# A gated recurrence feeding an attention mixture: mixing two experts per float32 product, the loads of V cut in halves, a shorter warm-up

## The chip, the cores and the metric

The kernel runs on one core of one Trainium2 chip. The metric is the device time of one execution in microseconds (us), the median of several runs. Five engines work side by side and meet at semaphores: PE (matrix products; its weight loads are listed as PEld), DVE (vector), ACT (scalar), POOL (a second, slower vector engine) and SP, which here only issues DMA transfers, in order.

## The reference

Six arrays of 4 batches x 8 heads x 768 steps x 40 go through a recurrence, and its output through a mixture of four attention experts of which each token takes two:

```
for t in range(S):                       # 768 steps, state 40 x 40 for each of 32 heads
    y[:, :, t] = rt @ state
    Sa = state @ at
    state = state * wt - outer(Sa, bt) + outer(vt, kt)
x = y as (4, 768, 320)
logits = x @ w_gate                      # 4 experts, the best 2 of each token
for e in range(4):
    q, k, v = x @ wq[e], x @ wk[e], x @ wv[e]          # 64 columns each
    a = softmax(causal(q @ k.T / 8))
    out += gate[e] * (a @ v @ wo[e])
```

## The kernel before

**Recurrence.** Time is cut into 24 chunks of 32 steps, and heads into 4 groups of 8, which makes 96 units (chunk `c`, group `g`). A unit has seven pieces, `s_k s_v s_g s_y s_f s_u s_t`, and the main loop runs over steps `n`: step n runs piece `k` of unit n+3, `v` of unit n-1, `g` of n, `y` of n-3, `f` of n-2, `u` of n and `t` of n-3, in that order (`MAIN`). Between the pieces stand jobs that a table places at a step and a slot: `prep` (scans and products that prepare decay factors, 24 of them, named by letters) and `invert` (32x32 triangular inverses on DVE and POOL, through DRAM). `R1` and `R2` hold operands of two chunks in turn. Rows 0 to 31 of both take V of the chunk from DRAM: `load_c(c, 0)` fills `R1` (read by `s_g`), `load_c(c, 1)` fills `R2[:, 0]` (read by `s_v` and `s_y`) and two more operands, `RB` and `RT`. Both are issued on SP at the end of steps n = 4m and 4m+2 for chunk m+1.

**Prologue.** Before the main loop `warm()` issues products on PE that nobody reads and four DVE operations on `LT`; then the line `START` prepares the first units and the first inverse.

**Mixture of experts.** `proj` makes queries, keys, values (`VV`) and gates of a batch, `unit(b, j, e, last)` handles 256 queries of expert `e`: `scores`, `transp` (PE transposes the weights, ACT and DVE bring them to `PT`), `mix` (PE multiplies `VV` with `PT` into `ot`), `fin` (output projection with float32 `WO`). Values and weights are held as a high and a low part of the type fp32r: `VV` has both side by side in 128 columns, `PT` has two tiles, so that a unit takes two products per block of keys and an addition afterwards (L841, L842). The order of units is the table `UNITS`; unit n+0 is scored, n-3 transposed, n-4 mixed and n-6 finished in one step (`LAG`), and `ORDER` says how these are interleaved. Work that waits a few slots goes through `later`.

## Time and profile before

| | |
|---|---|
| median of 3 runs | 747.99 us (745.74 to 750.92) |
| the profiled execution, its own time | 750.69 us |
| its span, first to last instruction | 748.8 us |
| busy: PE, DVE, ACT, POOL | 652.5, 583.1, 513.1, 335.6 us |
| mean granted clock of PE | 0.95 |

Busy time is the union of an engine's instructions; an engine that is 87% busy over the whole span may be the limit in one stage and wait in another, so the stages are read one by one. Three can be told apart: the prologue up to about 97 us, the recurrence to 490 us, the mixture to the end. A float32 product appears as two matmul records, an fp32r product as one.

### The profile page before, as it was taken

The page shows a single profiled execution, that of the slowest core. Times are in us where ns is not written, and L with a number is a line of the kernel's source. Part 1 is how long each engine was busy: PE and PEld are TensorE (multiplying, and loading weights), DVE is VectorE, ACT ScalarE, POOL GpSimd, SP SyncE. Part 2 cuts the span into 40 slices and gives each one's busy share as a digit, 9 for nine tenths or more (in the row PEclk, how much of TensorE's full clock was granted, in tenths as well). Part 3 has the DMA queues.
Part 4 walks back from the last instruction along what each step waited for, and adds up shares of the span by engine and source line. Part 5 has one row for each costly group of instructions (what it writes and reads, how often), then busy time and mean ns, then how long its engine had stood idle before and what let it go on. Part 6 is the DMA issues. An engine that isn't in the chain of part 4 may idle for free.

```text
span 748.8 us, 25460 instructions
## 1 busy us (share of the span) xinstructions
PE 652.5 (87%) x10321; PEld 600.2 (80%) x10321; DVE 583.1 (78%) x1436; ACT 513.1 (69%) x1270; POOL 335.6 (45%) x514
## 2 busy tenths in 40 slices
PE   6650699999899889988999999979979989999997
PEld 6540589888899879877999999967868878798785
DVE  8899869877886797789568344369999899789894
ACT  4697267667677776666567767627757768678784
POOL 4466368318803861486048002022555344523541
PEclk9565599999999999999999999999999999999999
DMA  7750634584478357834641661143213112111101
GB/s 197 192 141 15 131 105 117 126 190 124 110 162 220 82 126 158 204 90 111 126 138 58 140 188 49 49 130 95 47 47 103 50 33 75 57 40 43 37 19 57
DMA packets 87413, 78.27 MB, mean 105 GB/s; under 512 B 54392, under 2 KB 72568, under 8 KB 87288
## 3 DMA queue, kind: packets, MB, share of 16 engines
q1 hardware_dynamic: 87144, 76.47, 40.7%
q8 instruction: 83, 1.36, 0.8%
q14 instruction: 42, 0.34, 0.2%
q10 hardware_dynamic: 144, 0.10, 0.1%
HBM read 56.10 MB, written 14.16 MB: 94 GB/s over the span
## 4 chain that ended last, share of the span: by engine, by line
PE 54%; DVE 19%; DMA 10%; ACT 6%; issue 3%; SPq 1%; POOL 0%; DVEq 0%; ACTq 0%; POOLq 0%
DMA R<-in_VT 8%; PE ps L357 6%; PE ps L381 6%; PE ps L407 5%; PE ps L363 5%; PE ps L374 4%; PE ps L350 4%; PE ps L280 4%; PE ot L836 4%; PE pt L711 3%; PE sc L791 3%; PE pt L821 3%; PE pt L847 3%; PE ps L368 3%; DVE TP L310 3%
## 5 line engine op out<-in xcount | busy, mean ns | idle before, releaser
L813 POOL TENSOR_TENSOR P<-P,m 128x128 f32<-128x128 f32 (+2 forms) x96 | 89.2, 951 | 115.6 <-DVE m L809 53.7
L396 DVE TENSOR_TENSOR XT<-ps,SC 40x128 f32<-40x128 f32 x192 | 55.2, 287 | 76.7 <-ACT R L391 67.2
L312 POOL TENSOR_TENSOR MT<-MT,TP 128x58 f32<-128x58 f32 (+26 forms) x170 | 86.7, 510 | 13.3
L280 PE MATMUL ps<-AB,KB 104*64 104x64 f32 x768 | 63.1, 249 | 27.3 <-DVE PC L260 12.8
L364 ACT ACTIVATE R<-ps 32x320 f32<-32x320 f32 x96 | 41.0, 427 | 66.2 <-PE ps L363 66.1
L280 PEld LDWEIGHTS ps<-AB,KB 104*64 104x64 f32 x768 | 58.3, 163 | 28.8 <-POOL AB L267 13.7
L802 ACT ACTIVATE P<-sc,m 128x128 f32<-128x128 f32 (+2 forms) x96 | 60.9, 635 | 29.9 <-DVE m L801 19.2
L381 PE MATMUL ps<-R,LS 128*40 128x80 f32 x1536 | 75.8, 236 | 4.3 <-DVE R L375 4.1
L363 PE MATMUL ps<-GT,TT 128*33 128x40 f32 x1536 | 73.4, 205 | 3.7 <-DMA TT<-Td 1.5
L407 PE MATMUL ps<-CM,R 128*40 128x40 f32 x1472 | 75.9, 209 | 0.0
L363 PEld LDWEIGHTS ps<-GT,TT 128*33 128x33 f32 x1536 | 65.8, 115 | 4.9 <-ACT GT L358 2.8
L791 PE MATMUL sc<-ks,qs 128*128 128x384 f32 (+4 forms) x256 | 62.5, 346 | 4.7 <-ACT P L802 4.0
L836 PE MATMUL ot<-pt,vv 128*128 128x256 f32 (+1 forms) x384 | 60.3, 289 | 6.5 <-DVE ots L842 6.0
L407 PEld LDWEIGHTS ps<-CM,R 128*40 128x40 f32 x1472 | 64.6, 122 | 1.0 <-issue 0.9
L825 DVE TENSOR_TENSOR pt<-pt,pt 128x384 fp32r<-128x384 f32 (+1 forms) x96 | 58.9, 618 | 5.3 <-ACT pt L824 3.6
L381 PEld LDWEIGHTS ps<-R,LS 128*40 128x40 f32 x1536 | 58.1, 117 | 5.7 <-DVE R L375 5.2
L374 PE MATMUL ps<-RB,VU 128*64 128x64 f32 x768 | 61.2, 224 | 0.0
L836 PEld LDWEIGHTS ot<-pt,vv 128*128 128x128 f32 x384 | 50.8, 189 | 10.9 <-DVE ots L842 8.9
L801 DVE TENSOR_REDUCE m<-sc 128x1 f32<-128x128 f32 (+2 forms) x96 | 58.7, 614 | 0.6
L824 ACT ACTIVATE pt<-pt 128x384 fp32r<-128x384 f32 (+1 forms) x96 | 52.0, 544 | 10.0 <-PE pt L821 8.5
L821 PE MATMUL pt<-CM,P 128*128 128x128 f32 x336 | 52.9, 275 | 3.8 <-DVE qs L720 2.6
L368 PE MATMUL ps<-CM,R 66*80 66x66 f32 x384 | 38.7, 223 | 18.4 <-DMA R<-in_VT 17.8
(153 smaller groups left out, 1657.5 us busy)
## 6 DMA issues: line engine op xcount, KB each, us to landing
R<-in_VT SPq DMA_DIRECT2D x48, 160.0 KB
RB<-in_RB SPq DMA_DIRECT2D x24, 320.0 KB
EK<-in_EK SPq DMA_DIRECT2D x18, 416.0 KB
ks<-ks SPq DMA_DIRECT2D x32, 192.0 KB
R<-in_RT SPq DMA_DIRECT2D x24, 200.0 KB
EW<-in_EA SPq DMA_DIRECT2D x18, 214.5 KB
xT<-XT SPq DMA_DIRECT2D x48, 80.0 KB
out_dram<-o SPq DMA_DIRECT2D x24, 160.0 KB
```

Of the source, the lines that this page charges most:

```text
L280: T.matmul(p_a[:, p, cc, :], kb[0:104, n, :], AB[0:104, n, :], start=True, stop=True)
L312: lambda: e.tensor_tensor(o, o, tmp, op=OP.add)]
L363: T.matmul(p_u[:, h], tt[:, o:o + 33], gt[:, h, :], start=True, stop=True)
L368: T.transpose(p_t[:, p], r2[0:66, 0, h0 + 2 * p:h0 + 2 * p + 2, :].rearrange("q h d -> q (h d)"), ident[0:66, 0:66])
L374: T.matmul(p_f[:, 2 * p:2 * p + 2], vu[:, p, :], rb[:, 4 * g + p, :], start=True, stop=True)
L381: T.matmul(p_y[s][64 * s:64 * s + 40, p], ls[:, h, :], r2[:, :, h, :], start=True, stop=True, tile_position=(0, 64 * s))
L407: T.matmul(p_t[64:104, h], rn[:, h0 + h, :], ident[:, 64:104], start=True, stop=True, tile_position=(0, 64))
L791: T.matmul(ps[:, c, 0:cw], QS[b][:, e, o], KS[b][:, e, z, k], start=(z == 0), stop=(z == 1 and not last), skip_group_check=True)
L802: later(DE, lambda: A.activation(pv, ps[:, 0:ch, 0:cw], AF.Exp, bias=m[:, 0, t:t + 1], accum_out=m[:, 1, t:t + 1]))
L813: PL.tensor_tensor(P[:, 0:n], P[:, 0:n], m[:, 3, t:t + 1].to_broadcast([128, n]), op=OP.mult)
L821: T.transpose(p[:, 128 * y:128 * y + 128], st["P"][t][:, 128 * c:128 * c + 128], ident)
L836: T.matmul(po[:, 128:256] if one else po, VV[b][:, k, e].rearrange("p a b -> p (a b)"), PT[:, 256 * k:256 * k + (128 if one else 256)], st ...
```

## The change

Three things change. `warm()` keeps its first 48 products and drops the others and its four DVE operations. `load_c` has a third part, k == 2, which fills heads 0 to 15 of `R2`, and k == 1 fills heads 16 to 31; the loop issues parts 2 and 0 right after piece `y` of step 4m and part 1 right after `y` of step 4m+2. In the mixture `VV` and `PT` become plain float32, the two experts of a pair are mixed together, each into 64 of the 128 partitions of `ot` (`tile_position`), and one copy on DVE replaces L841 and L842. The copy to `PT` is on ACT for even blocks and on DVE for odd ones, without a low part. `UNITS` keeps pairs of experts adjacent, and a mix runs only at the second of a pair, all blocks in one go.

```diff
@@ load_c
+        if k == 2:
+            nc.sync.dma_start(R2[c % 2][0:32, 0, 0:16].rearrange("p h d -> p (h d)"), I["VT"][c, :, 0:640])
         if k == 1:
-            nc.sync.dma_start(R2[c % 2][0:32, 0].rearrange("p h d -> p (h d)"), I["VT"][c])
+            nc.sync.dma_start(R2[c % 2][0:32, 0, 16:32].rearrange("p h d -> p (h d)"), I["VT"][c, :, 640:1280])
@@ seq
-                load_c(int(z[1]), int(z[2]))
+                for k in (0,) if z[2] == "0" else (2, 1):
+                    load_c(int(z[1]), k)
@@ warm
-        z = [ps([128, 512]) for _ in range(4)]
...
-        run(48, lambda k: mm(128, 40, 80, 0, 64 * (k % 2), k % 2))
...
-        run(12, lambda k: mm(40, 40, 72, 64 * (k % 2), 64 * (k % 2), 0))
...
-        V.transpose(tv.rearrange("p (a b) -> p a b", a=4), c[:, None, :].to_broadcast([128, 4, 128]))
-        V.transpose(tv.rearrange("p (b a) -> p a b", a=16), c[:, None, 0:32].to_broadcast([128, 16, 32]))
-        V.memset(tv, 1.5)
-        V.reciprocal(tv, tv)
+        z = [ps([128, 512]) for _ in range(2)]
+        for k in range(48):
+            T.matmul(z[k % 2][64 * (k % 2):64 * (k % 2) + 40, 0:80], CM[:, 0:40], CM[:, 0:80], start=True, stop=True,
+                     tile_position=(0, 64 * (k % 2)))
@@ main loop, inside the loop over the pieces x of step n
-        if n >= 4:
-            if n % 4 == 0:
-                load_c(n // 4 + 1, 0)
-            if n % 4 == 2:
-                load_c(n // 4 + 1, 1)
+            if x == "y" and n >= 4:
+                for k in ((2, 0), (), (1,), ())[n % 4]:
+                    load_c(n // 4 + 1, k)
@@ proj, vg
-        VV[b] = sp.tile([128, 6, 4, 2, 64], FR, name="vv", bufs=2)
+        VV[b] = sp.tile([128, 6, 4, 64], F32, name="vv", bufs=2)
...
-                later(DL, lambda: V.tensor_tensor(v[:, :, 1], pv, f32(v[:, :, 0]), op=OP.subtract))
@@ unit, transp
-                st["PT"] = [sp.tile([128, 12, 128], FR, name=f"pt{x}", bufs=2) for x in range(2)]
+                PT[b, j, e] = sp.tile([128, 12, 128], F32, name="pt", bufs=4)
...
-            A.activation(h, p[:, 0:n], AF.Copy)
-            later(DL, lambda: V.tensor_tensor(l, p[:, 0:n], f32(h), op=OP.subtract))
+            if z % 2:
+                V.tensor_copy(o, p[:, 0:n])
+            else:
+                A.activation(o, p[:, 0:n], AF.Copy)
@@ unit, mix
-                for x in range(2):
-                    PT = st["PT"][x].rearrange("p a b -> p (a b)")
-                    T.matmul(po[:, 128:256] if one else po, VV[b][:, k, e].rearrange("p a b -> p (a b)"),
-                             PT[:, 256 * k:256 * k + (128 if one else 256)], start=(k == 0 and x == 0), stop=(one and x == 1),
-                             skip_group_check=True)
+                for s in range(2):
+                    h = slice(64 * s, 64 * s + 64)
+                    P = PT[b, j, 2 * ep + s].rearrange("p a b -> p (a b)")
+                    T.matmul(po[h, 128:256] if one else po[h], VV[b][:, k, 2 * ep + s], P[:, 256 * k:256 * k + (128 if one else 256)],
+                             start=(k == 0), stop=one, tile_position=(0, 64 * s), skip_group_check=True)
             if one:
                 ot = OT[b, j]
-                later(1, lambda: A.activation(ot[q, ep], po[64:128], AF.Copy))
-                later(2, lambda: V.tensor_tensor(ot[q, ep], po[0:64], ot[q, ep], op=OP.add))
+                later(1, lambda: V.tensor_copy(ot[:, ep], po))
```

Line numbers of the changed file: L836 is L818 there, L821 is L800, L791 is L770, L847 is L827, L711 is L692, L794 is L773, L336 and L337 are L338 and L339, and the halves of `R2` are L335 (first) and L337 (second).

DVE at the start of the program, before (`LT` is the tile that the four dropped operations write, `EW` the first input of the recurrence):

```order
L217 MEMSET D1P_83 104x528
L218 MEMSET AB_119 128x1024
L221 MEMSET FL 128x48
L500 STREAM_TRANSPOSE LT_125<-CM 128x512
L501 STREAM_TRANSPOSE LT_125<-CM 128x16x32
L502 MEMSET LT_125 128x512
L503 RECIPROCAL LT_125<-LT_125 128x512
L258 SCALAR_TENSOR_TENSOR SUF_84<-EW_80,D_78 104x528
```

DVE at the same place, after:

```order
L217 MEMSET D1P_83 104x528
L218 MEMSET AB_119 128x1024
L221 MEMSET FL 128x48
L258 SCALAR_TENSOR_TENSOR SUF_84<-EW_80,D_78 104x528
L260 COPY PC_85<-SUF_84 104x4
```

The first scan (L258) now follows the memsets directly.

SP in steps 4 to 8, before (`R_133` and `R_134` are the two buffers of `R1`, `R_135` and `R_136` those of `R2`; `EW`, `EK`, `EA` are inputs of `prep`):

```order
L199 DMA EK_82<-in_EK 104x1024
L199 DMA EA_81<-in_EA 104x512
L333 DMA R_133<-in_VT 32x1280
L199 DMA EW_80<-in_EA 104x528
L199 DMA EK_82<-in_EK 104x1024
L335 DMA R_135<-in_VT 32x1280
L336 DMA RB_139<-in_RB 80x1024
L337 DMA R_135<-in_RT 40x1280
L199 DMA EA_81<-in_EA 104x512
L199 DMA EW_80<-in_EA 104x528
L333 DMA R_134<-in_VT 32x1280
```

SP at the same place, after:

```order
L199 DMA EK_82<-in_EK 104x1024
L199 DMA EA_81<-in_EA 104x512
L335 DMA R_135<-in_VT 32x640
L333 DMA R_133<-in_VT 32x1280
L199 DMA EW_80<-in_EA 104x528
L199 DMA EK_82<-in_EK 104x1024
L337 DMA R_135<-in_VT 32x640
L338 DMA RB_139<-in_RB 80x1024
L339 DMA R_135<-in_RT 40x1280
L199 DMA EA_81<-in_EA 104x512
L335 DMA R_136<-in_VT 32x640
L333 DMA R_134<-in_VT 32x1280
```

The first half of `R2` now stands ahead of the load of `R1` and of two loads for `prep`; the second half keeps the place of the whole.

PE in the mixture, one unit of 256 queries with six blocks of keys, before (`pt_9831` and `pt_9832` are the high and the low tile of one expert):

```order
L821 MATMUL pt<-CM,P 128x128 x3
L836 MATMUL ot<-pt_9831,vv 128x256
L836 MATMUL ot<-pt_9832,vv 128x256
L836 MATMUL ot<-pt_9831,vv 128x256
L836 MATMUL ot<-pt_9832,vv 128x256
L836 MATMUL ot<-pt_9831,vv 128x256
L836 MATMUL ot<-pt_9832,vv 128x256
L836 MATMUL ot<-pt_9831,vv 128x256
L836 MATMUL ot<-pt_9832,vv 128x256
L836 MATMUL ot<-pt_9831,vv 128x256
L836 MATMUL ot<-pt_9832,vv 128x256
L836 MATMUL ot<-pt_9831,vv 128x128
```

PE in the mixture, a pair of experts with six blocks, after:

```order
L800 MATMUL pt<-CM,P 128x128 x3
L818 MATMUL ot<-pt,vv 64x256 x10
L818 MATMUL ot<-pt,vv 64x128 x2
L770 MATMUL sc<-ks,qs 128x320 x4
L773 LDWEIGHTS BF_6823
L773 MATMUL sc<-BF_6823 128x128
```

Twelve products on 64 partitions each now serve two experts, where twelve on 128 partitions served one.

## Rows read from the trace of the kernel before

**Rows 1.** The profile page: busy time and share of the span of each engine.

```profile
PE 652.5 (87%) x10321; PEld 600.2 (80%) x10321; DVE 583.1 (78%) x1436; ACT 513.1 (69%) x1270; POOL 335.6 (45%) x514
```

**Rows 2.** Busy time of each engine in stretches of the span (start and end in us, then the length, the engines, the granted clock, the DMA share and GB/s): the prologue, the recurrence, the mixture, and four stretches of 40 us inside the recurrence.

```profile
0.00:97.00 97.00, 50.81 (x696) 46.43 (x696) 87.57 (x189) 58.63 (x90) 49.45 (x65) 0.65 0.56 134
97.00:490.00 393.00, 367.19 (x8009) 348.45 (x8008) 274.24 (x664) 272.34 (x703) 176.02 (x327) 0.99 0.52 127
490.00:748.70 258.70, 234.52 (x1621) 205.30 (x1617) 221.31 (x584) 182.17 (x477) 110.16 (x122) 1.00 0.21 59
160.00:200.00 40.00, 35.92 (x763) 33.78 (x761) 31.40 (x70) 27.36 (x72) 31.24 (x50) 0.96 0.56 146
240.00:280.00 40.00, 34.77 (x763) 32.32 (x760) 34.41 (x81) 29.37 (x79) 31.28 (x58) 1.00 0.48 118
280.00:320.00 40.00, 36.34 (x796) 34.94 (x798) 28.31 (x63) 26.23 (x65) 12.87 (x18) 1.00 0.76 178
320.00:360.00 40.00, 33.91 (x718) 31.88 (x713) 35.14 (x79) 26.11 (x71) 27.27 (x48) 0.96 0.40 102
```

**Rows 3.** Instructions of DVE, SP and ACT in the first 20 us, in order of time (start, length, engine and line).

```profile
4.38 0.71 DVE L500 STREAM_TRANSPOSE LT<-CM 128x512 f32<-128x512 f32 x1 [1.40 <-DMA CM<-in_CM]
5.13 1.05 DVE L501 STREAM_TRANSPOSE LT<-CM 128x512 f32<-128x512 f32 x1
6.87 3.35 DVE L503 RECIPROCAL LT<-LT 128x512 f32<-128x512 f32 x1
10.14 1.19 DVE L258 TENSOR_TENSOR_SCAN SUF<-EW,D 104x528 f32<-104x528 f32 x1
15.36 1.24 DVE L258 TENSOR_TENSOR_SCAN TT<-R,D 104x528 f32<-104x528 f32 x1
...
4.79 0.31 SPq L199 DMA_DIRECT2D LS<-in_EA  x1
6.35 0.31 SPq L199 DMA_DIRECT2D R<-in_EA  x1
...
8.02 0.72 ACT L255 ACTIVATE JK<-EW,CM 104x512 fp8e4<-104x512 f32 x1
```

**Rows 4.** Waits (who waited for whom: us in total, times, longest): two of the whole span, then that of PE for the load of `R2` between 240 and 280 us and between 320 and 360 us.

```profile
PE ps L368 <- DMA R<-in_VT: 17.8, 10, 2.7
SPq L335 <- PE ps L381: 42.6, 5, 10.7
...
PE ps L368 <- DMA R<-in_VT: 4.7, 2, 2.7
PE ps L368 <- DMA R<-in_VT: 4.4, 2, 2.3
```

**Rows 5.** One of these waits in order of time: SP issues the whole load of `R2`, PE runs `s_k` (L350) and then waits to start `s_v` (L368).

```profile
188.61 0.35 SPq L335 DMA_DIRECT2D R<-in_VT  x1
...
190.93 0.55 PE L350 MATMUL ps<-CM,KB 104*64 104x104 f32 x4
194.19 0.40 PE L368 MATMUL ps<-CM,R 66*80 66x66 f32 x4 [2.71 <-DMA R<-in_VT]
```

**Rows 6.** The stretch behind that wait and the one after it: the columns of rows 2.

```profile
195.20:198.60 3.40, 3.40 (x58) 3.40 (x53) 2.73 (x8) 1.45 (x4) 2.93 (x7) 0.52 0.43 120
198.70:202.10 3.40, 3.40 (x81) 3.25 (x79) 2.88 (x8) 2.32 (x7) 2.82 (x8) 0.99 0.07 11
```

**Rows 7.** Groups of instructions of the mixture (490 to 749 us), shapes apart: busy us and mean ns of one, then idle time before them and its releaser. DVE first, then ACT, then PE.

```profile
L825 DVE TENSOR_TENSOR pt<-pt,pt 128x512 fp32r<-128x512 f32 x48 | 32.8, 685 | 1.7 <-ACT pt L824 0.7
L825 DVE TENSOR_TENSOR pt<-pt,pt 128x384 fp32r<-128x384 f32 x48 | 26.5, 551 | 3.6 <-ACT pt L824 2.9
L842 DVE TENSOR_TENSOR ots<-ot,ots 64x256 f32<-64x256 f32 x48 | 19.9, 415 | 4.8 <-ACT ots L841 3.9
L735 DVE TENSOR_TENSOR vv<-pt,vv 128x256 fp32r<-128x256 f32 x24 | 10.0, 420 | 1.3 <-ACT gg L734 0.9
...
L824 ACT ACTIVATE pt<-pt 128x512 fp32r<-128x512 f32 x48 | 28.6, 597 | 6.2 <-PE pt L821 5.6
L824 ACT ACTIVATE pt<-pt 128x384 fp32r<-128x384 f32 x48 | 23.6, 491 | 3.8 <-PE pt L821 2.9
L841 ACT ACTIVATE ots<-ot 64x256 f32<-64x256 f32 x48 | 18.3, 381 | 2.6 <-PE ot L836 1.3
...
L836 PE MATMUL ot<-pt,vv 128*128 128x256 f32 x288 | 51.7, 302 | 6.5 <-DVE ots L842 6.0 <-DVE gm L764 0.4
L847 PE MATMUL pt<-wo,ots 128*128 128x320 f32 x96 | 30.9, 443 | 0.0
L836 PE MATMUL ot<-pt,vv 128*128 128x128 f32 x96 | 16.3, 250 | 0.0
```

**Rows 8.** PE in order of time, in runs without a gap (start, from the first start to the last end, line, count): an fp32r mix, a float32 output projection, float32 products at the tile positions (0, 0) and (0, 64) in turn, unread products of 40 rows x 72 columns at the positions (0, 0) and (64, 64) in turn into one PSUM bank, and a change from 80 weight columns to 33.

```profile
692.67 1.59 PE L836 MATMUL ot<-pt,vv 128*128 128x256 f32 x12
650.76 1.24 PE L847 MATMUL pt<-wo,ots 128*128 128x320 f32 x4
126.90 0.72 PE L381 MATMUL ps<-R,LS 128*40 128x80 f32 x15
12.28 0.93 PE L487 MATMUL ps<-CM 40*40 40x72 f32 x24
138.11 0.40 PE L368 MATMUL ps<-CM,R 66*80 66x66 f32 x4 [0.68 <-DMA R<-in_VT]
138.44 0.33 PE L357 MATMUL ps<-R,GLe 128*33 128x40 f32 x4
```

**Rows 9.** The chain of work that ended last, inside the mixture: shares by line for 490 to 560 us, then for 560 to 735 us.

```profile
by line: ACT P L802 13.5%; issue 12.0%; DVE m L801 10.9%; DVE qs L720 6.5%; DMA x<-xT 5.9%; PE pt L711 4.5%; DVE vv L735 3.9%; DVE ks L720 3.6%; DVE xh L688 3.5%; DVE pt L825 3.5%; DVE gr L751 2.8%; DVE gr L753 2.5%; DVE gm L765 2.4%; DVE o
by line: PE ot L836 14.3%; PE sc L791 12.6%; PE pt L821 12.1%; PE pt L711 12.0%; PE pt L847 8.9%; PE pt L730 5.1%; issue 4.7%; DVE m L801 4.0%; ACT P L802 3.0%; DVE pt L825 2.9%; DVE qs L720 2.6%; DVE ots L842 2.6%; DVE m L807 2.0%; DMA x<-
```

More of the change, by code (lines that the diff above doesn't have):

```diff
@@ L479, in warm @@
     def warm():
-        z = [ps([128, 512]) for _ in range(4)]
-        c = CM[:, 0:128]
-        tv = LT.rearrange("p a b -> p (a b)")[:, 0:512]
-        def run(n, f):
-            for k in range(n):
-                f(k)
-        def mm(rows, m, n, r, q, b, o=0):
-            T.matmul(z[b][q:q + m, o:o + n], CM[r:r + rows, 0:m], CM[r:r + rows, 0:n], start=True, stop=True, tile_position=(r, q))
-        run(48, lambda k: mm(128, 40, 80, 0, 64 * (k % 2), k % 2))
-        run(16, lambda k: mm(32, 32, 40 - 2 * (k % 4), 32 * (k % 4), 32 * (k % 4), 0))
-        run(16, lambda k: mm(40, 32, 40 - 2 * (k % 8), 64 * (k % 2), 32 * (k // 2 % 4), k % 2))
-        run(16, lambda k: mm(40, 32, 32, 64 * (k % 2), 64 * (k % 2) + 32 * (k // 2 % 2), k % 2))
-        run(16, lambda k: mm(32, 40, 72 - 2 * (k % 8), 32 * (k // 2 % 4), 64 * (k % 2), k // 2 % 4))
-        run(12, lambda k: mm(40, 40, 32, 64 * (k % 2), 64 * (k % 2), 0))
-        run(12, lambda k: mm(40, 40, 72, 64 * (k % 2), 64 * (k % 2), 0))
-        run(8, lambda k: T.transpose(z[0][0:104, 0:128], c[:, 0:104], c))
-        run(8, lambda k: T.transpose(z[0][0:128, 0:104], c[0:104], c[0:104, 0:104]))
-        for k in range(8):
-            mm(32, 32, 40, 32 * (k % 4), 32 * (k % 4), 0)
-            mm(40, 40, 40, 64 * (k % 2), 64 * (k % 2), 1)
-        V.transpose(tv.rearrange("p (a b) -> p a b", a=4), c[:, None, :].to_broadcast([128, 4, 128]))
-        V.transpose(tv.rearrange("p (b a) -> p a b", a=16), c[:, None, 0:32].to_broadcast([128, 16, 32]))
-        V.memset(tv, 1.5)
-        V.reciprocal(tv, tv)
+        z = [ps([128, 512]) for _ in range(2)]
+        for k in range(48):
+            T.matmul(z[k % 2][64 * (k % 2):64 * (k % 2) + 40, 0:80], CM[:, 0:40], CM[:, 0:80], start=True, stop=True,
+                     tile_position=(0, 64 * (k % 2)))
     warm()
@@ L732, in f @@
                 pv = p[:, 0:256].rearrange("p (e d) -> p e d", e=4)
-                A.activation(v[:, :, 0], pv, AF.Copy)
+                A.activation(v, pv, AF.Copy)
                 A.activation(G[b][:, i], p[:, 256:260], AF.Copy)
-                later(DL, lambda: V.tensor_tensor(v[:, :, 1], pv, f32(v[:, :, 0]), op=OP.subtract))
             return f
@@ L771, in proj @@
                     H=lambda x: shift(half(x)), G=lambda x: gate(half(x)))
-    OT = {}
+    OT, PT = {}, {}
     def unit(b, j, e, last):
         ep, s = divmod(e, 2)
-        q = slice(64 * s, 64 * s + 64)
         st = {}
@@ L822, in transp @@
             n = 128 * len(k)
[L823 to L825 removed]
+            o = PT[b, j, e][:, 4 * z:4 * z + len(k)].rearrange("p a b -> p (a b)")
+            if z % 2:
+                V.tensor_copy(o, p[:, 0:n])
+            else:
+                A.activation(o, p[:, 0:n], AF.Copy)
         def mix(z):
             if z == 0:
[L828 removed]
+                st["o"] = pp.tile([128, 256], F32, name="ot", bufs=1)
                 if (b, j) not in OT:
                     OT[b, j] = sp.tile([128, 2, 256], F32, name="ots", bufs=6)
[L831 removed]
+            po = st["o"]
             for k in (2 * z, 2 * z + 1):
                 one = k == 2 * j + 1
[L834 to L838 removed]
+                for s in range(2):
[3 more added lines that the diff above has]
+                             start=(k == 0), stop=one, tile_position=(0, 64 * s), skip_group_check=True)
             if one:
                 ot = OT[b, j]
[L841 to L842 removed]
+                later(1, lambda: V.tensor_copy(ot[:, ep], po))
         def fin(t):
@@ L851, in fin @@
             later(1, lambda: nc.sync.dma_start(out[b, 128 * i:128 * i + 128], o))
-        return dict(s=scores, t=transp, v=mix, f=fin, nz=j + 1, last=last)
+        return dict(s=scores, t=transp, v=mix, f=fin, nz=j + 1, last=last, odd=s)
     if FL is not None:
@@ L888, in moe @@
         tt = [lambda z=z: ut["t"](z) for z in range(ut["nz"] if ut else 0)]
-        vv = [lambda z=z: uv["v"](z) for z in range(uv["nz"] if uv else 0)]
+        vv = [lambda z=z: uv["v"](z) for z in range(uv["nz"] if uv and uv["odd"] else 0)]
         ff = [lambda t=t: uf["f"](t) for t in range(2 if uf and uf["last"] else 0)] + (list(fill[n % 12]) if n < 48 else [])
@@ L894, in moe @@
         for x in ORDER:
-            pop(dict(s=ss, t=tt, m=vv, f=ff)[x])
+            for _ in range(len(vv) if x == "m" else 1):
+                pop(dict(s=ss, t=tt, m=vv, f=ff)[x])
         while vv or ff:
```

5 lines of the change are left out of this document (1 added, 4 removed).

## The prediction

> **What bounds the kernel now.** I began with the busy shares of the engines [rows 1]: PE leads with 87%, DVE follows with 78%, so neither is the limit everywhere. Then the busy times by stage [rows 2], from which the reader should take three things. In the prologue, up to 97 us, DVE is busy for 87.6 us and PE for half: DVE is the limit, and PE's clock, 0.65 on average there, prices little. In the recurrence PE is busy for 367.2 of 393 us, which leaves 25.8 us of idle PE. In the mixture PE has 234.5 and DVE 221.3 of 258.7 us: two engines near their limit, each waiting for the other. Next came the waits [rows 4], which say whom the idle PE waits for in the recurrence: 17.8 of the 25.8 us, in ten waits, are piece `s_v` waiting for V in `R2`. One of them in order of time [rows 5] shows why: SP issues the load at 188.61 us, and PE, ready since 190.93 + 0.55 us, starts L368 at 194.19. Last, the chain of waits inside the mixture [rows 9], to see which of the operations that go stand on it.
>
> **Prologue.** Four DVE operations go, and DVE's first scan, L258, starts at 10.14 us directly behind them [rows 3]. What it needs is `EW`. No row shows that load landing, but SP, whose ninth load is issued at 4.79 us and its tenth at 6.35, and ACT, which uses `EW` at 8.02, bracket it [rows 3]. It was issued first, so I take 4.8 us: 10.14 - 4.8 = 5.3 us, and by ACT's start at 8.02 as the latest end 2.1 us. The next inputs are far enough ahead, since the second scan (15.36 us) would move to 10.0 and SP was already free to issue that far down its list at 8 us. DVE has only 9.4 us of idle in these 97 us [rows 2], so what it gains at the front arrives at the end of the stage. The 120 unread products that go lie beside DVE's work and cost and give nothing; their cover is PE's half-idle prologue. Gain 5.3 us, ends 2.1 and 5.5.
>
> **Recurrence.** The first half of `R2` is issued two steps sooner; a step is 393 / 97 = 4.1 us, so it lands some 8 us before it did, against a longest wait of 2.7 us [rows 4]. The second half keeps its step but serves groups 2 and 3, whose `s_v` comes two steps later: again 8 us of slack more. The 24 extra issues on SP take 0.35 us each [rows 5] beside a queue that mostly waits. On SP the new first half waits for piece `y` of the same step, and behind it are queued the load of `R1` (needed at step 4m+4) and loads for `prep`; SP waited for `y` before too (L335 for L381, 42.6 us [rows 4]), so this is a wait moved, not made. All ten waits should go: 17.8 us. After a long one PE also runs at the lower of its two clock levels for 3.4 us, with 58 records against 81 in the next stretch of that length [rows 6], which is (81 - 58) / 81 x 3.4 = 1.0 us; twice by the dips in the granted clock, 2 us. Together 19.8 us as the upper end. What is late next is DVE: in two stretches of 40 us, from 240 and from 320 us, which hold 4.7 and 4.4 us of these waits [rows 4], DVE is busy for 34.4 and 35.1 us [rows 2], and 40 less the waits is 35.3 and 35.6. I expect half of these 9.1 us to turn into waits for DVE, so 19.8 - 4.6 = 15.2; the dips share in that, and I take 14. Lower end 8, if DVE takes back all of the 9.1 us and a share elsewhere.
>
> **Mixture, PE.** A float32 product costs more than an fp32r one, and this decides whether the change pays. Fp32r: twelve records in 1.59 us, the last 0.25 long, so eleven starts in 1.34 us over 10 x 256 + 128 = 2688 columns: 0.50 ns a column [rows 8, 7]. Float32: the output projection has 48 products but 96 records [rows 7], and four records start within 1.24 - 0.43 = 0.81 us, 0.27 us each; two records make 0.54 us for 320 columns, 1.69 ns a column [rows 8]. The mix before has 288 x 256 + 96 x 128 = 86016 columns [rows 7], 43.0 us. After, it has half the products, 43008 columns: 72.7 us one after the other, 36.3 us if the two experts run side by side. Do they? L381 uses the same two tile positions on float32 operands: 15 records in 0.72 us, the last 0.23 long, are 0.035 us a record, where 80 columns at the rate of the output projection would be 0.067 [rows 8]. So pairs at (0, 0) and (0, 64) do run side by side. There the two write different PSUM banks, here the same bank. The unread products of 72 columns wrote into one bank, and 24 records in 0.93 us are (0.93 - 0.22) / 23 = 0.031 us each against 0.061 [rows 8]; they differ in rows as well as columns, so it is a near row, not the same case. I take 36.3 us.
>
> Going into and out of half-width products may cost something. From L368 (80 weight columns) to L357 (33) the starts are 138.44 - 138.29 = 0.15 us apart, against 0.06 within L368 [rows 8]: 0.09 us a change. The mixes stand in 28 runs on PE, so 56 changes, 5 us. PE's own work is then 36.3 + 5 - 43.0, about 2 us less: nothing.
>
> The Trainium skill, "TensorEngine Tiling (Array Packing)", section "Tiling Modes" (Key Properties), says that changing the tiling mode drains the TensorE. Were a drain as long as one whole float32 record of L368 (about 0.22 us) the 56 changes would be an estimated 12 us instead of 5, and the sum 7 us later. The row at L368 shows less than half of that, and I go by the row.
>
> **Mixture, DVE and ACT.** DVE loses 96 subtractions (32.8 + 26.5 us), 48 additions (19.9) and 24 on the values (10.0): 89.2 us [rows 7]. It gains 32 copies of odd blocks, 16 of 512 and 16 of 384 columns; the nearest row is the subtraction of that shape out of PSUM, 16 x 0.685 + 16 x 0.551 = 19.8 us, and 24 copies of `ot`, by L842 24 x 0.415 = 10.0 us. Net 59 us less of 221. ACT loses L841 (18.3 us) and a third of L824 (16 x 0.597 + 16 x 0.491 = 17.4 us): 36 less of 182 [rows 2, 7]. What of it is on the path: in the chain L825 and L842 have 2.9 and 2.6% of 175 us, 9.6 us, and L735 and L825 3.9 and 3.5% of 70 us, 5.2 us [rows 9]. Together 14.8 us on the path. PE's 6.0 us of waiting for L842 go with it [rows 7], being the same time. What is late next is PE itself, busy for 234.5 us; its idle is 258.7 - 234.5 = 24.2 us [rows 2], of which start and end of the stage keep some 4, so 20 is the upper end. A burst of up to twelve float32 products, 2.4 us, holds back scores that DVE and ACT wait for, which takes a little back. I take 13. Lower end 0.
>
> **Sum.** 5.3 + 14 + 13 = 32.3 us. The profiled execution took 750.69 us by itself (span 748.8, and 1.9 around it), so it would be 718.4. It was 2.7 us above the median, and against the median of 747.99 the time is 715.7, rounded to 716.
>
> **Rivals.** *PE keeps the mixture where it is.* If L825 and L842 on the chain only stood for time that PE's next work would have taken anyway, the mixture gains nothing: 5.3 + 14 = 19.3 us, 729 us. For it speaks that PE is 91% busy there; against it that the chain of 560 to 735 us has DVE operations between the products. *DVE takes the place of the loads in the recurrence.* Then 8 instead of 14 us: 722 us. For it speak the two full stretches, against it that most of the other waits lie where DVE is less full (31.4 and 28.3 us of 40 from 160 and from 280 us [rows 2]). *The two experts of a pair are serialised*, because both write the same bank from the same rows. Then PE has 72.7 + 5 - 43.0 = 35 us more in a stage where it is already the busiest. Even if its idle time shrank by 10 us the mixture would be 25 us longer, and 748 + 25 - 14 = 759 us, slower than before (the gain in the recurrence at its lower end and the prologue's together taken as 14). The mix is worth 43008 / 512 = 84 pairs of products of 256 columns, 0.43 us a pair side by side; it decides from the point where a pair takes more than 0.43 + (14 + 10 + 2) / 84 = 0.74 us, since then PE's extra work eats the 14 us, the idle time and the 2 us saved. Against it speak L381 and the unread products into one bank. *The load does not do what it says*: SP is held up elsewhere and the first half is issued no sooner; then 5.3 + 13 = 18 us, 730 us. SP's in-order list speaks for it, two steps of slack against it.
>
> **How the numbers follow.** The forecast has 0.66, PE keeping the mixture 0.15, DVE in the recurrence 0.09, the load without effect 0.05, serialised pairs 0.05. The range takes the upper ends, 5.5 + 19.8 + 20 = 45 us, 703 us, and on the other side the case in which two terms stay at their lower ends, 5.3 + 8 + 0 = 13 us, 735 us; it leaves out the serialised pairs and the tails of the rest. About 1%, 7.5 us, is what a measurement of this kernel can tell from no change: faster is below 740.5 us, which all cases but one reach, with something taken off for combinations: 0.91; within 1% 0.04, slower 0.05.
>
> **What would show it.** In the profile after: L258 starting near 5 us; no wait of L368 for V; the granted clock without the dips near 195 and 356 us; the pairs L818 as twelve products in about 2.4 us; DVE near 160 us in the mixture, and PE's idle there well below 24 us. The prediction is wrong if the pairs take twice as long, if the recurrence gets new waits for DVE of more than 6 us, or if PE's idle in the mixture stays.

## The result and the profile after

The changed kernel took 725.3 us (median of 4 runs, 722.42 to 726.75) against 747.05 us for the kernel before beside it: a ratio of 0.968 with a 95% interval of 0.964 to 0.972. The two medians alone give 0.971, inside that interval; a fourth run of the kernel before moved its median from the 747.99 us that the prediction started from. Some executions of a kernel fall into a slower state, and the medians and ratios below leave them out: three of twelve of e4_units, one each of e10_order and e11_late. The prediction was 716 us with a range of 703 to 735. The direction and the range held; the forecast was 9 us too hopeful.

The profiled execution took 726.4 us, its span is 724.4. For a fair split I cut both spans at two instructions: the first product on `y` (L381 before, L383 after) of the first unit, and that of the last unit. These are the busy times by stage at these cuts, first of the kernel before and then of the changed one (the columns are those of [rows 2]):

```profile
0.00:99.20 99.20, 52.95 (x734) 48.19 (x735) 88.03 (x190) 59.85 (x93) 49.52 (x66) 0.66 0.57 138
99.20:489.40 390.20, 364.45 (x7961) 346.16 (x7960) 273.78 (x662) 271.12 (x701) 175.96 (x327) 0.99 0.52 126
489.40:748.80 259.40, 235.12 (x1633) 205.82 (x1633) 221.31 (x584) 182.17 (x477) 110.16 (x122) 1.00 0.21 59
```

```profile
0.00:94.40 94.40, 46.25 (x512) 43.20 (x513) 83.04 (x186) 59.66 (x93) 49.56 (x65) 0.62 0.60 147
94.40:470.90 376.50, 361.11 (x7961) 343.65 (x7957) 274.09 (x662) 270.04 (x700) 180.38 (x327) 1.00 0.51 130
470.90:724.40 253.50, 236.87 (x1633) 188.49 (x1633) 174.68 (x472) 147.91 (x397) 108.60 (x122) 0.99 0.22 61
```

Read the second number of each row: the prologue is 4.8 us shorter, the recurrence 13.7, the mixture 5.9; together the 24.4 us by which the spans differ. Forecast were 5.3, 14 and 13. So nearly the whole miss lies in the mixture, 7.1 us of 7.9. There DVE has 47 us less to do and ACT 34, and yet PE's busy time has gone up from 235.1 to 236.9.

The page's line of busy times, which answers [rows 1], says the same for the whole span, PE at 89% and DVE down from 78 to 73%:

```profile
PE 644.2 (89%) x10097; PEld 575.3 (79%) x10097; DVE 531.8 (73%) x1320; ACT 477.6 (66%) x1190; POOL 338.5 (47%) x514
```

**Prologue.** DVE in order of time, to be held against [rows 3]. The first scan L258 starts at 4.12 us instead of 10.14, and what it waits for is named: the load of `EW`, the bound that was open between 4.8 and 8.02 us. The second scan starts at 9.54, forecast 10.0.

```profile
2.88 0.10 DVE L221 MEMSET FL<- 128x48 f32 x1
4.12 1.26 DVE L258 TENSOR_TENSOR_SCAN SUF<-EW,D 104x528 f32<-104x528 f32 x1 [1.14 <-DMA EW<-in_EA]
...
9.54 1.24 DVE L258 TENSOR_TENSOR_SCAN TT<-R,D 104x528 f32<-104x528 f32 x1
```

**Recurrence.** No wait of `s_v` for the load of V is left. In its place stands a wait for DVE, and SP's wait has moved with the loads; the lines answer to [rows 4] (both of the whole span). The same wait of PE for DVE had been 4.1 us in 7 waits before (shown first), so 9.6 us have come.

```profile
PE ps L381 <- DVE R L375: 4.1, 7, 0.8
```

```profile
PE ps L383 <- DVE R L377: 13.7, 16, 1.6
SPq L335 <- PE ps L383: 47.6, 16, 7.0
```

**Mixture.** The groups with shapes apart, of PE and of DVE, answer to [rows 7], and the run of one mix on PE in order of time to [rows 8]:

```profile
L818 PE MATMUL ot<-pt,vv 128*64 128x256 f32 x288 | 39.4, 391 | 0.0
L818 PE MATMUL ot<-pt,vv 128*64 128x128 f32 x96 | 11.2, 280 | 0.0
```

```profile
L804 DVE COPY pt<-pt 128x512 f32<-128x512 f32 x16 | 10.9, 682 | 0.9 <-PE pt L800 0.8
L822 DVE COPY ots<-ot 128x256 f32<-128x256 f32 x24 | 10.1, 420 | 11.2 <-PE ot L818 11.2
L804 DVE COPY pt<-pt 128x384 f32<-128x384 f32 x16 | 8.8, 553 | 2.5 <-PE pt L800 2.5
```

```profile
559.18 0.60 PE L800 MATMUL pt<-CM,P 128*128 128x128 f32 x4
559.72 2.60 PE L818 MATMUL ot<-pt,vv 128*64 128x256 f32 x24
562.24 0.55 PE L800 MATMUL pt<-CM,P 128*128 128x128 f32 x3
```

Twelve products are 24 records in 2.60 us, for two experts; before, two experts took 2 x 1.59. The copies cost what was forecast (19.7 and 10.1 us). What the reader should look at is the idle time behind the bar: DVE now stands idle before L822 because PE has not finished the mix, 11.2 us, where before PE had stood idle for DVE's L842, 6.0 us [rows 7]. Likewise DVE's reduction L780 waits for PE's scores:

```profile
DVE m L780 <- PE sc L773: 26.6, 40, 2.1
```

In the chain from 540 to 712 us the operations of DVE that went are gone, and PE's have filled their room; before, L836, L791, L821 and L847 had 14.3, 12.6, 12.1 and 8.9% of 560 to 735 us [rows 9]:

```profile
by line: PE ot L818 19.8%; PE sc L770 14.2%; PE pt L800 13.2%; PE pt L827 12.8%; PE pt L692 9.4%; PE pt L711 5.4%; ACT P L781 3.1%; DVE m L780 2.8%; DMA x<-xT 2.4%; issue 2.1%; PE sc L773 2.0%; ACT qs L700 1.9%; DVE ks L701 1.9%; DVE gc L72
```

### The profile page after: what moved, and what is told of

Same layout as the page of the kernel before. It is cut to its first block, busy times and chain, and to the rows that moved or that the text cites. A ratio compares the mean times of both kernels' runs of the same rounds, so it can differ in the third digit from the quotient of the medians.

```text
span 724.4 us, 24783 instructions
## 1 busy us (share of the span) xinstructions
PE 644.2 (89%) x10097; PEld 575.3 (79%) x10097; DVE 531.8 (73%) x1320; ACT 477.6 (66%) x1190; POOL 338.5 (47%) x514
## 4 chain that ended last, share of the span: by engine, by line
PE 63%; DVE 21%; ACT 6%; issue 2%; DMA 1%; SPq 0%; DVEq 0%; ACTq 0%
PE ps L383 6%; PE ps L359 6%; PE ps L409 6%; PE ps L365 6%; PE ot L818 5%; PE ps L280 5%; PE ps L376 5%; PE ps L352 4%; PE sc L770 4%; PE pt L692 4%; DVE TP L310 4%; PE pt L800 4%; PE pt L827 3%; DVE MT L312 3%; PE pt L711 3%
## 5 line engine op out<-in xcount | busy, mean ns | idle before, releaser
L792 POOL TENSOR_TENSOR P<-P,m 128x128 f32<-128x128 f32 (+2 forms) x96 | 87.6, 935 | 104.0 <-DVE m L788 47.9
L312 POOL TENSOR_TENSOR MT<-MT,TP 128x58 f32<-128x58 f32 (+26 forms) x170 | 88.7, 522 | 13.3
L383 PE MATMUL ps<-R,LS 128*40 128x80 f32 x1536 | 75.0, 235 | 13.7 <-DVE R L377 13.7
L780 DVE TENSOR_REDUCE m<-sc 128x1 f32<-128x128 f32 (+2 forms) x96 | 59.4, 622 | 27.8 <-PE sc L773 26.6
L383 PEld LDWEIGHTS ps<-R,LS 128*40 128x40 f32 x1536 | 57.6, 117 | 15.9 <-DVE R L377 15.8
L770 PE MATMUL sc<-ks,qs 128*128 128x384 f32 (+4 forms) x256 | 64.1, 351 | 4.9 <-ACT P L781 4.6
L393 ACT ACTIVATE R<-ps 40x160 f32<-40x160 f32 x144 | 42.7, 297 | 17.9 <-PE ps L383 10.7
L310 POOL TENSOR_TENSOR TP<-LT,MT 128x210 f32<-128x210 f32 (+29 forms) x101 | 50.3, 498 | 7.8
L376 PEld LDWEIGHTS ps<-RB,VU 128*64 128x64 f32 x768 | 53.7, 139 | 0.1
L800 PE MATMUL pt<-CM,P 128*128 128x128 f32 x336 | 52.3, 277 | 1.4 <-ACT pt L806 1.1
L352 PE MATMUL ps<-CM,KB 104*64 104x104 f32 x384 | 53.4, 264 | 0.0
L312 DVE TENSOR_TENSOR MT<-MT,TP 128x108 f32<-128x108 f32 (+34 forms) x151 | 48.6, 334 | 2.9
```

The costliest lines, as they stand in the source:

```text
L310: return [lambda: e.tensor_tensor(tmp, row[:, None, :].to_broadcast([128, m, n]), M[:, r0:r0 + m, j][:, :, None].to_broadcast([128, m, n]) ...
L312: lambda: e.tensor_tensor(o, o, tmp, op=OP.add)]
L352: T.transpose(p_k[:, 2 * p:2 * p + 2].rearrange("q s e -> q (s e)")[:, 0:104], kb[0:104, p * 4 + cw, :], ident[0:104, 0:104])
L376: T.matmul(p_f[:, 2 * p:2 * p + 2], vu[:, p, :], rb[:, 4 * g + p, :], start=True, stop=True)
L383: T.matmul(p_y[s][64 * s:64 * s + 40, p], ls[:, h, :], r2[:, :, h, :], start=True, stop=True, tile_position=(0, 64 * s))
L770: T.matmul(ps[:, c, 0:cw], QS[b][:, e, o], KS[b][:, e, z, k], start=(z == 0), stop=(z == 1 and not last), skip_group_check=True)
```

## The experiments

All stand in this table, cut at the same two instructions; "mixture" is the end less the second cut. The ratio is to the kernel before on the same chip; its median was 747.05 us beside the changed kernel and 746.3 to 750.45 beside the experiments.

| kernel | median us | ratio (95%) | first `y` | last `y` | span | mixture | PE busy in it |
|---|---|---|---|---|---|---|---|
| before | 747.05 | 1 | 99.2 | 489.4 | 748.8 | 259.4 | 235.1 |
| changed | 725.3 | 0.968 (0.964–0.972) | 94.4 | 470.9 | 724.4 | 253.5 | 236.9 |
| e1_warm | 737.54 | 0.985 (0.980–0.990) | 90.0 | 475.7 | 735.8 | 260.1 | 235.1 |
| e2_load | 736.62 | 0.983 (0.978–0.988) | 98.8 | 474.9 | 734.3 | 259.4 | 235.0 |
| e3_mix | 741.04 | 0.988 (0.983–0.993) | 99.2 | 486.8 | 740.2 | 253.4 | 235.4 |
| e4_units | 750.83 | 1.003 (1.000–1.007) | 95.6 | 482.4 | 746.0 | 263.6 | 241.1 |
| e5_nolow | 745.55 | 0.996 (0.992–0.999) | 95.7 | 486.2 | 743.0 | 256.8 | 234.2 |
| e6_spread | 728.38 | 0.971 (0.966–0.976) | 93.7 | 470.2 | 727.4 | 257.2 | 240.7 |
| e7_serial | 740.89 | 0.990 (0.985–0.995) | 90.0 | 467.4 | 738.9 | 271.5 | 256.1 |
| e8_fewer | 720.17 | 0.961 (0.957–0.966) | 90.0 | 467.2 | 714.9 | 247.7 | 225.4 |
| e13_places | 726.16 | 0.967 (0.964–0.970) | 93.8 | 471.6 | 725.4 | 253.8 | 236.5 |
| e10_order | 721.38 | 0.965 (0.961–0.969) | 93.6 | 470.7 | 719.4 | 248.7 | 233.4 |
| e11_late | 720.02 | 0.967 (0.963–0.971) | 90.0 | 466.6 | 718.1 | 251.5 | 235.4 |
| e12_both | 716.9 | 0.963 (0.959–0.966) | 90.0 | 466.6 | 715.4 | 248.8 | 233.7 |

### Each part alone, put into the kernel before

**The warm-up.** Only `warm()` is changed.

```diff
-        run(48, lambda k: mm(128, 40, 80, 0, 64 * (k % 2), k % 2))
...
-        V.reciprocal(tv, tv)
+        for k in range(48):
+            T.matmul(z[k % 2][64 * (k % 2):64 * (k % 2) + 40, 0:80], CM[:, 0:40], CM[:, 0:80], start=True, stop=True,
```

> The kernel before with the shorter warm-up alone. If DVE's order at the front is what the prologue waits for, L258 starts near 4.1 us instead of 10.1 and the whole gains 5 to 6 us (ratio about 0.993). Rival: the dropped products kept PE's clock up for the first units, and the gain is lost again by step 0: 0 to 2 us.

**The load.** Only `load_c` and its calls.

```diff
+        if k == 2:
+            nc.sync.dma_start(R2[c % 2][0:32, 0, 0:16].rearrange("p h d -> p (h d)"), I["VT"][c, :, 0:640])
...
+            if x == "y" and n >= 4:
+                for k in ((2, 0), (), (1,), ())[n % 4]:
+                    load_c(n // 4 + 1, k)
```

> The kernel before with the halved and earlier load of V alone. If the ten waits of L368 go and about a third of them turns into waits for DVE, 12 to 13 us less (ratio about 0.983); 18 us (0.976) if nothing takes their place; 0 if SP issues the halves no sooner.

**The mixture.** Float32 `VV` and `PT`, the pairs, and the new `UNITS`, with the old warm-up and load.

```diff
+                PT[b, j, e] = sp.tile([128, 12, 128], F32, name="pt", bufs=4)
...
+                             start=(k == 0), stop=one, tile_position=(0, 64 * s), skip_group_check=True)
```

> The kernel before with the float32 mix of two experts and its order of units alone. By the trace of after the mixture gains about 6 us (ratio 0.992); by the prediction it was 13 us (0.983). Were the stages not additive, the sum of the three parts alone would miss the 22 us of the whole by more than 3 us.

Measured by their ratios, the three save 11, 12.5 and 8.5 us, more together (32) than the whole change (22 to 24). The table shows some of the overlap. The mixture alone gives 259.4 - 253.4 = 6.0 us, just what it gives inside the change (5.9). So the small gain there is its own; neither the load nor the warm-up took it.

The warm-up's 11 us are not all its own. Its first `y` is at 90.0 us where the changed kernel, with the same warm-up, has 94.4; and among kernels with the old warm-up and the old load it is 99.2 (before, e3_mix) or 95.6 to 95.7 (e4_units, e5_nolow), with nothing changed ahead of it. What differs is the granted clock (the third number from the right, 0.50 or 1.00), from 78.8 to 93.4 us first in the changed kernel, then in e7_serial, which has the same prologue:

```profile
78.80:93.40 14.60, 13.48 (x135) 12.04 (x134) 10.89 (x15) 7.16 (x16) 2.01 (x2) 0.50 0.49 122
```

```profile
78.80:93.40 14.60, 12.78 (x234) 11.07 (x232) 13.10 (x19) 10.79 (x26) 3.47 (x4) 1.00 0.59 154
```

PE is nearly always busy in both, and 135 of its records fall into this stretch at the lower of its two levels, 234 at the higher. Like against like the warm-up is worth 95.7 - 90.0 = 5.7 us, or 99.2 - 94.4 = 4.8: the 5.3 us forecast. The one profile of before fell on the late rise.

The 98.8 us of e2_load have another cause. Its clock rose early, for its first `y` ran at the higher level, but PE paused for 5.07 us among the unread products of the old warm-up, waiting for nothing that the profile shows ("issue"). The products behind the pause ran to 25.8 us, and DVE's L281 had to wait 4.45 us for the first product after them. Here are these unread products and L281 in the kernel before, and then in e2_load (L490 is L487 there):

```profile
11.66 1.54 PE L487 MATMUL ps<-CM 32*40 32x58 f32 x49 [0.74 <-issue]
22.77 0.66 DVE L281 TENSOR_TENSOR GLe<-ps,CM 64x512 f32<-64x512 f32 x1
```

```profile
16.81 2.65 PE L490 MATMUL ps<-CM 32*40 32x58 f32 x49 [5.07 <-issue]
27.30 0.68 DVE L281 TENSOR_TENSOR GLe<-ps,CM 64x512 f32<-64x512 f32 x1 [4.45 <-PE ps L280]
```

The first `y` then stands 3.2 us later than in e4_units (98.8 against 95.6). So the products that the change drops can cost something: 3.2 us in this one of the five profiles that have them. Whether the edit of the load brought the pause is not shown.

The other share of the warm-up's 11 us is in the recurrence (385.7 us against 390.2), and goes with a shorter wait for V. PE's wait for the load was 12.0 us in e1_warm's profile:

```profile
PE ps L368 <- DMA R<-in_VT: 12.0, 8, 2.7
```

In the five profiles with the old load it was 12.0, 13.5, 14.1, 16.9 and 17.8 us, and their recurrences lasted 385.7, 387.6, 386.8, 390.5 and 390.2 us: the stage follows the wait, and the profile that I read had the largest. In the kernels with the new load the recurrence lasts 376.1 to 377.8 us, whatever else they change. So the load is worth 8 to 14 us, 11.3 on the mean (388.2 - 376.9). Which of the two does it, the halving or the earlier issue, was not separated.

These readings come from one profile of each kernel. By its ratio, from six executions, the warm-up saves 7.5 to 15 us, and the 4.8 to 5.7 us of the prologue lie below that. How often the late rise, the pause of PE or a short wait for V falls on either kernel no run here shows, so the rest of the 11 us stays open.

### What holds the mixture

**The new order of units alone**, in the kernel before.

```diff
-UNITS = ("00 01 02 03 10 11 12 13 23 21 20 22", "20 10 00 21 11 01 22 12 02 23 13 03", "00 10 11 23 20 22 21 13 01 12 03 02")
+UNITS = ("00 01 02 03 10 11 12 13 20 21 22 23", "20 21 10 11 00 01 22 23 12 13 02 03", "20 21 22 23 10 11 00 01 12 13 02 03")
```

> The kernel before with the new order of units alone, mixing unchanged. If the order that keeps pairs adjacent is worse by itself, 3 to 7 us slower, and this is where the missing 7 us of the mixture went. Rival: PE's own work bounds the mixture, the order is worth nothing, within 1.5 us of before.

The mixture grew by 4.2 us (263.6 against 259.4), the kernel by 0 to 0.7%. This is an edit that my sum had no term for. The rows show the whole mixture, then a stretch in it and the one behind:

```profile
482.40:746.00 263.60, 241.11 (x1633) 209.97 (x1633) 222.34 (x584) 182.65 (x477) 109.96 (x122) 0.98 0.21 59
494.30:497.70 3.40, 3.40 (x12) 3.40 (x12) 3.26 (x18) 1.19 (x3) 1.60 (x3) 0.50 0.01 3
497.70:542.10 44.40, 40.67 (x274) 36.06 (x274) 42.26 (x131) 32.01 (x93) 19.90 (x30) 1.00 0.27 72
```

The growth is not idle time of PE, which fell from 24.3 to 22.5 us. PE's busy time grew by 6.0 us with the same 1633 records. Three times in this mixture the granted clock fell to 0.50 for 3.4 us, and PE has 12, 12 and 15 records there, where the rate of the third row would give 21. That costs an estimated (9 + 9 + 6) / 21 x 3.4 = 3.9 us, nearly all of the growth, and the mixture of the kernel before has no such dip ahead of its last products. Whether the new order brings the dips or this one profile happened to have them is not shown.

**DVE's low parts alone.** In the kernel before, without L825; both products read the high tile, so that the high part is added twice.

```diff
-            later(DL, lambda: V.tensor_tensor(l, p[:, 0:n], f32(h), op=OP.subtract))
...
-                    PT = st["PT"][x].rearrange("p a b -> p (a b)")
+                    PT = st["PT"][0].rearrange("p a b -> p (a b)")
```

> The kernel before without the low part of the softmax weights on DVE (L825, 96 subtractions, 59 us of DVE): the two products of a block both read the high tile, so PE's work is the same and the result lacks the low part. If DVE's work was worth the 13 us of the prediction, 10 to 15 us less (ratio 0.980 to 0.987). If PE's own work bounds the mixture, 3 to 7 us less (0.991 to 0.996).

```profile
486.20:743.00 256.80, 234.18 (x1633) 205.62 (x1633) 174.67 (x488) 180.42 (x477) 109.55 (x122) 1.00 0.21 60
```

DVE's busy time falls by 46.6 us, as much as in the change, PE's work stays, and the mixture is 2.6 us shorter (the kernel 0.4%, 0.1 to 0.8). My chain had L825 on it with 2.9% of 175 us and 3.5% of 70 us, 7.5 us in sum [rows 9]. It gave a third of that.

**No bursts.** The changed kernel with one pair of blocks of a mix in each place of `ORDER`, not all at once.

```diff
-            for _ in range(len(vv) if x == "m" else 1):
-                pop(dict(s=ss, t=tt, m=vv, f=ff)[x])
+            pop(dict(s=ss, t=tt, m=vv, f=ff)[x])
```

> The changed kernel with the mix of a pair cut into its blocks of two, one in each place of the order, instead of all in one go. If the burst of up to twelve float32 products holds back the scores that DVE and ACT wait for, 3 to 6 us less than the changed kernel. If PE's work is the bound, no gain, and up to 4 us more for some 40 further changes of width at about 0.1 us.

The mixture is 3.7 us longer (257.2), with 3.8 us more of PE's busy time, and the kernel about 3 us slower (0.971 against 0.968, with intervals that overlap). So the bursts do not hold it back. Spread out, the mixes stand in 41 runs on PE where they stood in 28, which is 26 more changes into or out of half width; if nothing else made the difference, a change costs 3.8 / 26 = 0.15 us.

**The experts one after the other.** The changed kernel with all products of the first expert ahead of those of the second.

```diff
-            for k in (2 * z, 2 * z + 1):
-                one = k == 2 * j + 1
-                for s in range(2):
+            for s in range(2 if z == 0 else 0):
+                for k in range(2 * j + 2):
+                    one = k == 2 * j + 1
```

> The changed kernel with all products of the first expert of a pair ahead of all of the second, so that neighbours use the same half of the array. By the prediction's rates the mix then takes 73 instead of 36 us of PE, and with PE as the bound the time is 30 to 36 us above the changed kernel, slower than before. If PE has slack, 10 to 20 us above it.

A full mix then takes 4.38 us where it took 2.60:

```profile
558.83 4.38 PE L818 MATMUL ot<-pt,vv 128*64 128x256 f32 x24
```

PE's busy time rises by 19.2 us (256.1) and the mixture by 18.0: work added to PE comes out at the end nearly one for one. It also settles that the pairs of the changed kernel do run side by side, though both write one PSUM bank.

**Less work for PE.** The changed kernel without the products of the low part of `x` in the projections, 112 of them.

```diff
-        return [(w[0][:, k], h[:, k]) for k in range(3)] + [(w[1][:, k], h[:, k]) for k in range(3)] + \
-               [(w[0][:, k], l[:, k]) for k in range(2)]
+        return [(w[0][:, k], h[:, k]) for k in range(3)] + [(w[1][:, k], h[:, k]) for k in range(3)]
```

> The changed kernel without the two products with the low part of x in each projection of the mixture (112 products of 512 left out; the result lacks that part). It takes 64 x 0.175 + 48 x 0.12 = 17 us off PE and nothing off DVE and ACT. If PE's own work bounds the mixture, 12 to 17 us less than the changed kernel; if the chain through DVE and ACT does, less than 6.

PE's busy time falls by 11.5 us, the mixture by only 5.8. In three parts, cut at the same scores, first the changed kernel and then this one:

```profile
470.90:516.00 45.10, 41.38 (x280) 35.66 (x280) 35.67 (x115) 27.30 (x83) 18.63 (x29) 1.00 0.40 107
516.00:682.00 166.00, 159.54 (x1109) 127.97 (x1108) 121.37 (x304) 101.08 (x262) 76.10 (x76) 0.99 0.19 54
682.00:724.40 42.40, 35.96 (x248) 24.86 (x247) 17.64 (x54) 19.53 (x55) 13.87 (x18) 0.97 0.11 38
```

```profile
467.20:514.30 47.10, 40.35 (x236) 32.46 (x236) 37.51 (x115) 27.27 (x83) 18.82 (x29) 0.89 0.48 127
514.30:672.70 158.40, 149.00 (x1040) 117.79 (x1038) 121.30 (x303) 100.73 (x262) 75.95 (x76) 0.99 0.18 49
672.70:714.90 42.20, 36.01 (x248) 24.90 (x247) 17.71 (x54) 19.58 (x56) 13.88 (x18) 0.99 0.11 38
```

In the middle, where PE of the changed kernel is busy for 159.5 of 166 us and DVE for 121, 10.5 us less of PE's work shorten the stage by 7.6. At the start 44 products fewer gain nothing: a load of `x` stands on the chain there, where the chain of the changed kernel has none, the granted clock falls to 0.89, and 2.0 us are lost.

```profile
470.58 4.83 DMA x<-xT
```

So in the middle of the mixture the time follows PE's own work, and at its start it does not.

### Putting the order back

Here the new order is undone in the two middle batches only. A pair must then wait for its second expert, so `PT` needs six places. A second kernel has the six places alone.

```diff
-UNITS = (..., "20 21 10 11 00 01 22 23 12 13 02 03", ...)
+UNITS = (..., "20 10 00 21 11 01 22 12 02 23 13 03", ...)
...
-                PT[b, j, e] = sp.tile([128, 12, 128], F32, name="pt", bufs=4)
+                PT[b, j, e] = sp.tile([128, 12, 128], F32, name="pt", bufs=6)
```

> The changed kernel with one thing put back: the two middle batches take their units in the order of the kernel before (the three blocks in turn, one chunk after the other) and not in the new one, and the buffer of transposed attention has six places instead of four so that a pair of blocks can wait for each other. The mixture in float32, the warm-up and the halved load stay. Theory one, that the new order took back part of what the mixture gave (the new order alone cost the mixture 4.2 us in the kernel before, 263.0 against 258.7): the mixture comes to 249 to 251 us, against 252.9, and the kernel to 721 to 724 us. Theory two, that PE's own work bounds the mixture and the order is of no matter: 252 to 254 us and 724 to 727 us.

> The changed kernel with only the buffer of transposed attention at six places instead of four; the units keep their new order. The run with the earlier order of the middle batches had both, and its mixture took 248.7 us against 252.9. If the order was what made the difference, the mixture stays at 252 to 254 us and the kernel, by its ratio to the kernel before, where the changed kernel is (0.968). If the two further places were, the mixture comes to 248 to 250 us and the ratio to 0.963 or so.

The mixture with the earlier order:

```profile
470.70:719.40 248.70, 233.38 (x1633) 187.13 (x1633) 173.34 (x472) 148.85 (x397) 109.36 (x122) 0.99 0.22 62
```

The places alone leave it at 253.8 us (ratio 0.967); the order makes it 248.7. The two profiles part between the 33rd and the 49th product of L773: 36.5 us here, 43.7 in the changed kernel. In that stretch (the changed kernel first, then this one) PE is idle for 2.9 us against 0.7, and the granted clock is 0.96 against 1.00, one dip of 3.4 us at 592 us. The changed kernel also holds 27 more of PE's records there, work that this one does later, so only a part of the 7.2 us is a gain:

```profile
562.80:606.50 43.70, 40.81 (x289) 33.52 (x288) 30.86 (x83) 24.77 (x70) 16.07 (x19) 0.96 0.23 62
```

```profile
563.20:599.70 36.50, 35.78 (x262) 30.37 (x260) 27.33 (x78) 24.59 (x67) 17.56 (x18) 1.00 0.21 60
```

DVE's wait for scores (26.6 us above) is 16.3 in this kernel:

```profile
DVE m L780 <- PE sc L773: 16.3, 30, 1.6
```

By the ratio to before, 0.965 against 0.968 and 0.967, the gain is within what the intervals leave open; the stage shows it, the whole time alone does not. Its size depends on the profiles compared. The mixture is 253.5, 253.8, 253.4 and 251.5 us with the new order (changed, e13_places, e3_mix, e11_late) and 248.7 and 248.8 with the earlier one (e10_order, e12_both). The first two have the dip of the clock and the others none ahead of their last products, so between e11_late and e12_both the order and the places are worth 2.7 us, between the changed kernel and e10_order 4.8.

### Keeping PE busy ahead of the first units

The changed kernel with 80 more unread products behind the first product on the gates of unit 0, and then with both additions.

```diff
-    0: "/7d//7q/6nm 5o/6q/7m",
+    0: "/7d//7q W/6nm 5o/6q/7m",
...
+            elif z == "W":
+                warm(1, 80)
```

> The changed kernel with 80 more unread products on PE, of the form of the 48 of the warm-up, put behind the first product on the gates of unit 0, where PE has little to do from 64 to 75 us of the span; the 48 stay. Theory one, that the last of the prologue hangs on when the granted clock rises (the same program began the recurrence's first product on y at 90.0 us where it rose at 78.7, and at 93.7 to 94.4 where it rose at 93.6): with PE kept busy the rise comes ahead of the first units in every run, the first product on y at 89 to 91 us, and the median falls by 2 to 4 us, to 721 to 723. Theory two, that the rise does not answer to these products: 724 to 727 us, or a little over where they stand in the way of unit 0.

> The changed kernel with both: the earlier order of the middle batches and the 80 later unread products. If both gains are there and add up: 717 to 721 us. If neither is: 724 to 728 us. If only one is, 720 to 724 us, by which of the two single kernels is faster.

The stretch from 78.8 to 93.4 us in e11_late:

```profile
78.80:93.40 14.60, 13.13 (x234) 11.38 (x233) 13.10 (x20) 10.85 (x26) 3.11 (x4) 0.97 0.64 169
```

It is at the higher level here, and the first `y` stands at 90.0 us in both profiles. But e1_warm, e7_serial and e8_fewer had 90.0 without these products, so two profiles do not show that they bring the rise about in every run, and e11_late's ratio (0.967) is the changed kernel's. With both additions the median is 716.9 us (716.12 to 720.91), ratio 0.963: 0.6 of a per cent under the changed kernel, with intervals that overlap a little. In the profiles it is 9.0 us under it, 4.4 before the first `y`, which is the early rise, and 4.7 in the mixture, part of which is the dip. It is the best version I ran; that it beats the kernel before is certain, that it beats the changed one is likely.

## Why the prediction was right in two stages and wrong in the third

**Prologue, 5.3 forecast: right.** 4.8 to 5.7 us, by the step as worked out: DVE's start is what moved, the load of `EW` is what now comes last (4.12 us, the estimate was 4.8), and DVE's gain arrived at the end of the stage. That the unread products "cost and give nothing" was not tested apart from DVE's four operations, and in e2_load's profile they cost 3.2 us. That PE's clock "prices little" in the prologue was wrong: the first `y` stands at 90.0 us or at 93.6 to 94.4 by the time at which the clock rises.

**Recurrence, 14 forecast: right by the profile (13.7), a little high on the mean (11.3), and in part by luck.** The ten waits for the load went (17.8 us), and 9.6 us of waits for DVE came where I expected 4.6. More than 6 us was named as a sign that the prediction is wrong, and this term of the sum was: DVE took back more than half of what the load gave. Two things made up for it. PE's busy time fell by 3.3 us (364.45 to 361.11; the granted clock went from 0.99 to 1.00), where the dips had been given 2, and some 2 us of other waits of PE went (its idle time fell by 10.4 us in all). Also, the 17.8 us came from a profile in which the wait was the largest of five.

**Mixture, 13 forecast, 5.9 measured: two steps failed.** The first is an edit without a price. "`UNITS` keeps pairs of experts adjacent" is in the diff, and the sum has no term for it. Undone in the middle batches of the changed kernel it gives 2.7 to 4.8 us by stage; put alone into the kernel before it cost 4.2, nearly all of it in dips of the clock that it may not have caused. With the earlier order in those batches the mixture gives 259.4 - 248.7 = 10.7 us.

The second is the size of "what of it is on the path". PE's own work came out as forecast, about 2 us less: 233.4 against 235.1 us of busy time with the earlier order. Its idle time fell by 9.0 us (24.3 to 15.3), not by 13. I had counted L825's 7.5 us of the chain in full; taken away alone it gave 2.6. The rival that PE keeps the mixture had the right reason for that (such a row stands partly for time that PE's next work takes anyway) and the wrong size: it allowed no gain at all. Which of the other removals, L841 and L842, L735 or ACT's third of L824, gave the remaining 8 us was not separated. DVE was to come down to about 160 us in the mixture and has 174.7: the busy times of its groups add up to 246 us before and 189 after, 57 less where 59 were forecast, but neighbouring records overlap, and the busy time of the stage, from which I took the 59, fell by 47.

**A burst of float32 products takes a little back**: it did not; spreading it cost 3 to 4 us. **Entering and leaving half width, 0.09 us for each of 56 changes, 5 us**: by e6_spread rather 0.15 us each, 8 us, as far as the spreading changed nothing else. That lies between the row at L368 (0.09) and the length of one float32 record there (0.22). The Trainium skill, "TensorEngine Tiling (Array Packing)", section "Tiling Modes", says that changing the tiling mode drains the TensorE; e6_spread agrees in that 26 more changes came with 3.8 us more of PE's busy time.

**The serialised pairs** were the case on the other side. e7_serial, which comes near it, took 0.990 of the time before: even then the load and the warm-up would have kept the kernel ahead. The 759 us were too dark, since the change of expert still overlaps and a full mix takes 4.38 us and not twice 2.60.

## What to carry to other kernels

An operation's share of the chain of waits need not be what its removal gives (here 7.5 us on the chain, 2.6 us gained): hold it against the busy share of the engine whose work stands next, and try it alone before it is summed. Price every line of a diff, an order table too; here the order that made room for a good change took back a quarter to nearly half of what the mixture could give, and could be undone for the middle of the work. Before a difference between two profiles is put down to an edit, compare the granted clock of the two stretches. And take a wait from several profiles when it is the largest term: the same recurrence waited 12 to 18 us for the same load in five profiles.
